# Plain loads with casts on GpSimd, and the first batch transposed by TensorE, in an attention and long-convolution kernel

## Chip, cores, metric

One NeuronCore of a Trainium2 chip. The time is that of one execution on the device, in microseconds (us), as a median of several executions; a profile is one execution with the hardware's records. Some executions are slower than the others whatever the kernel, and are marked slow. The times given are medians of fast runs.

## The reference, cut to what matters

q, k and v are (4 batches, 8 heads, 768 positions, 64), float32. Five heads see only four sink positions and a window of 64; three see every earlier position. The attention output of a batch, 768 x 512, goes through a projection to three parts, a convolution of the middle part with a filter along the sequence, two multiplications and an output projection:

```python
a = softmax(mask(q @ k.T / 8))              # causal, or causal and (sink or window)
x = (a @ v).transpose(0, 2, 1, 3).reshape(4, 768, 512)
x1, x2, x3 = split(x @ w_proj, 3)
x2_conv = irfft(rfft(x2, axis=1) * rfft(filter_fft, axis=0))
out = (x1 * x2_conv * x3) @ w_out           # float32, (4, 768, 512)
```

## The kernel before

The kernel works on pairs: one batch and two heads, 16 in all, four to a batch. A pair needs q and k with the 64 channels on the partitions (`qkT`), and v with positions on the partitions. Scores go through an exponential on ScalarE into `pT`, VectorE multiplies 11 of the 21 blocks of 128 x 128 by a mask of zeros and ones, TensorE multiplies with v (`v_aug`, or `v_far` where v itself is masked). `attn` is transposed into `xT`, and with four pairs done the feed-forward part of that batch (`moe`, with the convolution as matrix products) runs interleaved with the next batch's attention. The parts that the change touches:

```python
def emit_loads(b, hp):
    qk = ald.tile([128, 2, NT, 2, D], BF16, name="qk")
    vf = ald.tile([128, 2, NT, D], FP32, name="v_f32")
    for a, src in ((0, q), (1, k)):
        for hh in range(2):                      # the DMA casts float32 to bfloat16
            nc.gpsimd.dma_start(out=qk[:, a, :, hh],
                in_=src[b, 2 * hp + hh].rearrange("(t p) d -> p t d", p=128))
    nc.sync.dma_start(out=vf, in_=v[b, 2 * hp:2 * hp + 2].rearrange("h (t p) d -> p h t d", p=128))
    return qk, vf
...
def emit_v(st):                                  # cut
    nc.vector.tensor_copy(out=v_aug[:, :, :, 0:64], in_=vf.rearrange("p hh t d -> p t hh d"))
    nc.gpsimd.tensor_mul(v_far, v_aug[:, 0:4], vmask[...])

def emit_prep(st):                               # the crossbar transposes 12 blocks of 128 x 128
    nc.sync.dma_start_transpose(out=qkT.rearrange("p a (t s) -> p (a t) s", t=NT),
                                in_=loads[st["pair"]][0].rearrange("p a t hh d -> p (a t hh d)"))

def emit_turn(st):                               # attn to xT: TensorE for the last pair only,
    if st is state[len(pairs) - 1]: ...          # else the crossbar, 6 blocks
```

"Crossbar" is the DMA transpose. In the code a DMA on `nc.sync` is issued by SyncE (SP), one on `nc.gpsimd` by GpSimd (POOL). A scheduler puts the instructions of each engine into an order, guided by the order of the program.

The softmax here doesn't subtract the row's maximum and nothing guards it: scores larger than these inputs give would overflow.

## Time and profile before

| | before |
|---|---|
| time | 268.87 us (268.46 to 269.48, 3 runs) |
| profiled span | 268.2 us |
| first exponential | 16.61 us |
| feed-forward of batch 0, 1, 2, 3 starts at | 82.4, 135.4, 184.8, 229.3 us |
| granted TensorE clock before the first of these | 0.80 of full speed |
| packets of all DMA queues | 121,523 |

I call the first of these starts **S1**. It divides the kernel: ahead of it transfers bound, behind it TensorE is busy over 90% until the tail. The slices, the chain and the table by stage are in the prediction. One more line sums the first part up. In the page's table of groups, a line has busy time and mean duration before the second bar, and after it the idle time of the engine ahead of these instructions with what ended it:

```profile
L287 PE MATMUL sc<-qkT 64*128 64x512 bf16 (+3 forms) x256 | 37.4, 342 | 42.9 <-DMA qkT<-qk 34.3
```

TensorE stood still for 34.3 us because the transposed q and k had not landed.

### The profile page before, as it was taken

The numbers are of one execution on the slowest core, as the hardware profiler recorded it, in microseconds if no ns is written. First come the engines' busy times: TensorE is split into PE (matmuls) and PEld (weight loads), VectorE is DVE, ScalarE is ACT, GpSimd is POOL, SyncE is SP. The second block draws the span as 40 slices with busy tenths as digits, with TensorE's granted clock in tenths as the row PEclk, the third lists the DMA queues.
The fourth block names the chain that finished last, engine by engine and source line by source line (L and its number), as shares of the span: only waits on it lengthen the run. The fifth ranks groups of instructions, "written<-read, shape, count | busy, mean of one in ns | idle before, by whom it ended". The sixth has DMA issues, their size and how long they took to land.

```text
span 268.2 us, 4095 instructions
## 1 busy us (share of the span) xinstructions
PE 199.7 (74%) x1598; PEld 98.2 (37%) x1598; DVE 153.3 (57%) x290; ACT 152.8 (57%) x182; POOL 80.6 (30%) x118
## 2 busy tenths in 40 slices
PE   0031800729757998998899999999999997999980
PEld 0010500414331434445343455544445462446520
DVE  1329610337743489569944984994397487055640
ACT  1059710445931786766778877768886631664331
POOL 8926940164455155160605426101010000000000
PEclk9999965568955999999999999999999999999997
DMA  8999999999999398999999699748410100410005
GB/s 131 143 172 200 178 169 196 172 163 159 155 180 65 61 148 82 145 142 105 130 302 158 93 136 166 82 87 201 124 29 2 29 4 0 190 47 1 0 7 228
DMA packets 121523, 32.06 MB, mean 120 GB/s; under 512 B 115616, under 2 KB 118432, under 8 KB 121504
## 3 DMA queue, kind: packets, MB, share of 16 engines
q0 software_dynamic: 53072, 9.18, 50.3%
q1 hardware_dynamic: 68432, 22.62, 46.8%
q8 instruction: 12, 0.20, 0.3%
q14 instruction: 7, 0.06, 0.1%
HBM read 24.65 MB, written 6.29 MB: 115 GB/s over the span
## 4 chain that ended last, share of the span: by engine, by line
PE 42%; DVE 21%; DMA 17%; ACT 11%; POOL 4%; issue 3%; ACTq 0%; POOLq 0%; DVEq 0%
DMA qkT<-qk 14%; PE x_ps L378 12%; PE x_ps L346 8%; PE att L313 6%; PE out_ps L407 6%; PE sc L287 5%; ACT pT L293 4%; PE X_ps L216 4%; DVE pT L300 4%; POOL qk L100 3%; DVE conv L399 3%; DVE y L401 2%; DVE conv L400 2%; DVE m L365 2%; DMA xT<-attn 2%
## 5 line engine op out<-in xcount | busy, mean ns | idle before, releaser
L293 ACT ACTIVATE pT<-sc 128x1024 bf16<-128x1024 f32 x96 | 85.8, 923 | 47.1 <-PE sc L287 46.6
L287 PE MATMUL sc<-qkT 64*128 64x512 bf16 (+3 forms) x256 | 37.4, 342 | 42.9 <-DMA qkT<-qk 34.3
L100 POOL DMA_DIRECT2D qk<-in_q_dram x32 | 26.9, 843 | 68.2 <-DMA qkT<-qk 65.0
L378 PE MATMUL x_ps<-xT,wproj 128*128 128x384 bf16 x256 | 46.7, 326 | 0.8 <-ACT X L360 0.8
L300 DVE TENSOR_TENSOR pT<-pT,mask 128x1024 bf16<-128x1024 bf16 x32 | 25.8, 806 | 28.2 <-ACT pT L293 28.2
L313 PE MATMUL att<-v_aug,pT 128*128 128x65 bf16 x352 | 36.3, 206 | 7.3 <-DVE pT L300 4.2
L313 PEld LDWEIGHTS <-pT 128*128 128x128 bf16 x672 | 28.8, 105 | 24.8 <-DVE pT L300 8.4
L287 PEld LDWEIGHTS <-qkT 64*128 64x128 bf16 x256 | 11.8, 98 | 68.7 <-DMA qkT<-qk 34.8
L378 PEld LDWEIGHTS <-wproj 128*128 128x128 bf16 x256 | 23.2, 98 | 16.2 <-issue 3.1
L346 PE MATMUL x_ps<-wproj,xf 128*128 128x512 bf16 x96 | 24.3, 402 | 4.3 <-DVE xf L339 4.2
L100 POOL DMA_DIRECT2D qk<-in_k_dram x32 | 27.0, 850 | 0.2
L407 PE MATMUL out_ps<-wout,y 128*128 128x512 bf16 x96 | 23.9, 381 | 3.8 <-DVE y L401 2.4
L313 PE MATMUL att<-v_far,pT 128*128 128x65 bf16 x320 | 25.9, 206 | 0.0
L216 PE MATMUL X_ps<-x,G 128*128 128x512 bf16 x96 | 23.6, 379 | 0.6 <-ACT X L355 0.3
L268 POOL TENSOR_TENSOR v_far<-v_aug,vmask 128x520 bf16<-128x520 bf16 x16 | 18.8, 1175 | 11.7 <-DVE v_aug L265 11.6
L410 ACT COPY o_sb<-out_ps 128x1024 f32<-128x1024 f32 x12 | 12.2, 1013 | 14.7 <-PE out_ps L407 11.5
L385 ACT CAST x1s<-x_ps 128x768 bf16<-128x768 f32 x16 | 12.8, 800 | 13.5 <-PE x_ps L378 13.5
L349 ACT CAST x<-x_ps 128x1024 bf16<-128x1024 f32 x12 | 12.2, 1014 | 13.0 <-PE x_ps L346 12.8
L365 DVE TENSOR_TENSOR m<-X,HAB 128x1024 bf16<-128x1024 bf16 x12 | 9.8, 815 | 16.1 <-ACT X L355 16.1
L387 DVE TENSOR_TENSOR g<-x1s,x_ps 128x768 bf16<-128x768 bf16 x16 | 15.2, 949 | 6.5 <-PE x_ps L378 5.0
L394 PE MATMUL c_ps<-Gi,P 128*128 128x384 bf16 x96 | 17.6, 326 | 1.5 <-DVE g L387 1.2
L298 DVE TENSOR_TENSOR pT<-pT,mask 128x512 bf16<-128x512 bf16 x16 | 6.7, 416 | 20.0 <-ACT pT L293 20.0
(70 smaller groups left out, 202.8 us busy)
## 6 DMA issues: line engine op xcount, KB each, us to landing
v_f<-in_v_dram SPq DMA_DIRECT2D x16, 384.0 KB, 5.4
out_dram<-o_sb SPq DMA_DIRECT2D x12, 512.0 KB, 2.9
qk<-in_q_dram POOLq DMA_DIRECT2D x32, 96.0 KB, 5.5
qk<-in_k_dram POOLq DMA_DIRECT2D x32, 96.0 KB, 6.2
wproj<-in_moe_w_proj_dram POOLq DMA_DIRECT2D x3, 512.0 KB, 13.1
filt<-in_moe_filter_fft_dram POOLq DMA_DIRECT2D x1, 768.0 KB, 11.4
wout<-in_moe_w_out_dram POOLq DMA_DIRECT2D x1, 512.0 KB, 17.1
qkT<-qk SPq DMA_TRANSPOSE x16, 5.0
```

The costliest lines, as they stand in the source:

```text
L100: nc.gpsimd.dma_start(out=qk[:, a, :, hh], in_=src[b, 2 * hp + hh].rearrange("(t p) d -> p t d", p=128))
L216: nc.tensor.matmul(ps[:, u, :], lhsT=G[:, m, t, :], rhs=src[:, r, m, :], start=(m == 0), stop=(m == NM - 1))
L268: nc.gpsimd.tensor_mul(v_far, v_aug[:, 0:4], vmask[:, hp, :, :, None].to_broadcast([128, 4, 2, 65]))
L287: nc.tensor.matmul(sc[:, hh, n * 128:(n + cnt) * 128], lhsT=qkT[rows, 1, j * 128:(j + 1) * 128], rhs=qkT[rows, 0, i * 128:(i + cnt) * 128] ...
L293: nc.scalar.activation(out=pT[:, :, 512 * c:512 * c + w], in_=sc[:, :, 0:w], func=AF.Exp, scale=SCALE)
L300: nc.vector.tensor_mul(near[:, :, c - 1:c + 1, 0:256], near[:, :, c - 1:c + 1, 0:256], mask[:, h0:h0 + 2, 1, None, :].to_broadcast([128, 2 ...
L313: nc.tensor.matmul(att[:, i, :], lhsT=st["pT"][:, hh, at:at + 128], rhs=st["v_far" if i >= j + 2 else "v_aug"][:, j, hh, :], start=(j == 0 ...
L346: nc.tensor.matmul(ps[:, r, :], lhsT=xf[:, cc, r, m * 128:(m + 1) * 128], rhs=wproj[:, cc, DM:2 * DM], start=(cc == 0), stop=(cc == NC - 1))
L378: nc.tensor.matmul(ps[:, s, 0:HS], lhsT=wproj[:, cc, part * DM + cb * 128:part * DM + (cb + 1) * 128], rhs=xT[:, cc, s * HS:s * HS + HS], ...
L387: nc.vector.tensor_mul(g[:, cb, :].rearrange("p (s t) -> p s t", s=2), x1s, halves[1])
L394: nc.tensor.matmul(ps[:, r, 0:HS], lhsT=P[:, t, u, ch], rhs=Gi[:, :, tile_no, :], start=(n == 0), stop=(n == 2))
L407: nc.tensor.matmul(ps[:, n, :], lhsT=y[:, cb, (i + n) * 128:(i + n + 1) * 128], rhs=wout[:, cb, :], start=(cb == 0), stop=(cb == NC - 1))
```

## The change

Its intent: shorten the first 80 us. Loads of q and k become plain float32 loads from SyncE with GpSimd casting afterwards; for the four pairs of batch 0 the rows are six positions wide (1536 bytes instead of 256) and TensorE transposes q, k and the attention output; the weights are asked for only after the casts of pairs 2, 3 and 4. The diff, cut (the flags of the heads, computed later in the setup, are left out):

```diff
+    def emit_loads(n):
+        qk = ald.tile([128, 2, 2, NT, D], FP32, name="qk_f32")
+        rows = "h (p t) d -> p h t d" if n < BY_PE else "h (t p) d -> p h t d"
+        for dst, src, order in ((qk[:, 0], q, rows), (qk[:, 1], k, rows), (vf, v, "h (t p) d -> p h t d")):
+            nc.sync.dma_start(out=dst, in_=src[b, 2 * hp:2 * hp + 2].rearrange(order, p=128))
+    BY_PE = 4
-    def emit_loads(b, hp):            # four casting loads on GpSimd, v on SyncE
+    def emit_cast(st):
+        for a in range(2):
+            engine = nc.vector if st["n"] == 0 and a == 0 else nc.gpsimd
+            st["cast"] = engine.tensor_copy(out=st["bf"][:, a], in_=qk[:, a].rearrange("p hh t d -> p t hh d"))
     def emit_prep(st):
+        if st["n"] < BY_PE:
+            for a in range(2):
+                ps = bank("qkT_ps", [128, S], BF16)
+                for t in range(NT):
+                    nc.tensor.transpose(ps[:, t * 128:(t + 1) * 128], ..., identity)
+                dst = qkT[:, a].rearrange("d (p t) -> d p t", t=NT)
+                src = ps.rearrange("d (t p) -> d p t", t=NT)
+                # a == 0: copied by VectorE, a == 1: by ScalarE
+            return
         nc.sync.dma_start_transpose(...)
     def emit_v(st):
-        nc.vector.tensor_copy(out=v_aug[:, :, :, 0:64], ...)
+        nc.gpsimd.tensor_copy(out=v_aug[:, :, :, 0:64], ...)
     def emit_turn(st):
-        if st is state[len(pairs) - 1]:
+        if st["n"] < BY_PE or st["n"] == len(pairs) - 1:
     # filter, projection, output weights: issued in pairs 1, 2, 3 instead of 0 and 1, each
+                with tc.issue_after(nxt["cast"].ins):
```

A table load for the sine was moved to the very start as well.

More of the change, by code (lines that the diff above doesn't have):

```diff
@@ L88 @@
     pairs = [(b, hp) for b in range(B) for hp in range(HP)]
-    state.update((n, {"pair": pp}) for n, pp in enumerate(pairs))
+    state.update((n, {"pair": pp, "n": n}) for n, pp in enumerate(pairs))
+    def emit_loads(n):
+        b, hp = pairs[n]
+        qk = ald.tile([128, 2, 2, NT, D], FP32, name="qk_f32")
+        vf = ald.tile([128, 2, NT, D], FP32, name="v_f32")
+        rows = "h (p t) d -> p h t d" if n < BY_PE else "h (t p) d -> p h t d"
+        for dst, src, order in ((qk[:, 0], q, rows), (qk[:, 1], k, rows), (vf, v, "h (t p) d -> p h t d")):
+            nc.sync.dma_start(out=dst, in_=src[b, 2 * hp:2 * hp + 2].rearrange(order, p=128))
+        return qk, vf
@@ L92 @@
+    BY_PE = 4
+    loads = {0: emit_loads(0)}
     ret_i64 = const.tile([128, H], mybir.dt.int64, name="ret_i64")
     nc.sync.dma_start(out=ret_i64, in_=is_retrieval.partition_broadcast(128))
-    def emit_loads(b, hp):
-        qk = ald.tile([128, 2, NT, 2, D], BF16, name="qk")
-        vf = ald.tile([128, 2, NT, D], FP32, name="v_f32")
-        for a, src in ((0, q), (1, k)):
-            for hh in range(2):
-                nc.gpsimd.dma_start(
-                    out=qk[:, a, :, hh], in_=src[b, 2 * hp + hh].rearrange("(t p) d -> p t d", p=128))
-        nc.sync.dma_start(
-            out=vf, in_=v[b, 2 * hp:2 * hp + 2].rearrange("h (t p) d -> p h t d", p=128))
-        return qk, vf
@@ L106, with emit_prep @@
-    PREFETCH = 2
-    loads = {pp: emit_loads(*pp) for pp in pairs[:1]}
+    def emit_cast(st):
+        qk = loads[st["n"]][0]
+        st["bf"] = asb.tile([128, 2, NT, 2, D], BF16, name="qk_bf")
+        for a in range(2):
+            engine = nc.vector if st["n"] == 0 and a == 0 else nc.gpsimd
+            st["cast"] = engine.tensor_copy(out=st["bf"][:, a], in_=qk[:, a].rearrange("p hh t d -> p t hh d"))
+    def emit_prep(st):
+        st["qkT"] = qkT = asb.tile([128, 2, S], BF16, name="qkT")
+        if st["n"] < BY_PE:
+            for a in range(2):
+                ps = bank("qkT_ps", [128, S], BF16)
+                for t in range(NT):
+                    nc.tensor.transpose(ps[:, t * 128:(t + 1) * 128],
+                                        st["bf"][:, a, t].rearrange("p hh d -> p (hh d)"), identity)
+                dst = qkT[:, a].rearrange("d (p t) -> d p t", t=NT)
+                src = ps.rearrange("d (t p) -> d p t", t=NT)
+                if a == 0:
+                    nc.vector.tensor_copy(out=dst, in_=src)
+                else:
+                    nc.scalar.copy(out=dst, in_=src)
+            return
+        nc.sync.dma_start_transpose(
+            out=qkT.rearrange("p a (t s) -> p (a t) s", t=NT),
+            in_=st["bf"].rearrange("p a t hh d -> p (a t hh d)"))
@@ L110 @@
     setup_order = tc.manual_schedule(engines={mybir.EngineType.DVE, mybir.EngineType.Pool})
     setup_order.__enter__()
+    table = const.tile([128, 1], FP32, name="table")
+    nc.vector.memset(table, 0.0)
+    nc.scalar.activation(out=table, in_=table, func=AF.Sin)
     G = const.tile([128, NM, 8, 128], BF16, name="G")
@@ L140 @@
     )
-    ret_w = const.tile([128, 2 * H], FP32, name="ret_w")
-    nc.vector.tensor_scalar(out=ret_w, in0=ret_i64.bitcast(I32), scalar1=0.0, scalar2=None,
-                            op0=ALU.not_equal)
-    ret = const.tile([128, H], FP32, name="ret")
-    nc.vector.tensor_max(ret, ret_w[:, 0:2 * H:2], ret_w[:, 1:2 * H:2])
     nc.gpsimd.affine_select(
@@ L166 @@
                                 op0=ALU.mult)
+    emit_cast(state[0])
     for m in range(NM):
@@ L177 @@
                              scale=-ETA)
+    emit_prep(state[0])
+    ret_w = const.tile([128, 2 * H], FP32, name="ret_w")
+    nc.vector.tensor_scalar(out=ret_w, in0=ret_i64.bitcast(I32), scalar1=0.0, scalar2=None,
+                            op0=ALU.not_equal)
+    ret = const.tile([128, H], FP32, name="ret")
+    nc.vector.tensor_max(ret, ret_w[:, 0:2 * H:2], ret_w[:, 1:2 * H:2])
     if n_sink:
@@ L261, in emit_v @@
     def emit_v(st):
-        vf = loads.pop(st["pair"])[1]
+        vf = loads.pop(st["n"])[1]
         st["v_aug"] = v_aug = asb.tile([128, NT, 2, 65], BF16, name="v_aug")
         nc.gpsimd.memset(v_aug[:, :, :, 64:65], 1.0)
-        nc.vector.tensor_copy(out=v_aug[:, :, :, 0:64], in_=vf.rearrange("p hh t d -> p t hh d"))
+        nc.gpsimd.tensor_copy(out=v_aug[:, :, :, 0:64], in_=vf.rearrange("p hh t d -> p t hh d"))
         st["v_far"] = v_far = asb.tile([128, 4, 2, 65], BF16, name="v_far")
@@ L268, in emit_v @@
         nc.gpsimd.tensor_mul(v_far, v_aug[:, 0:4], vmask[:, hp, :, :, None].to_broadcast([128, 4, 2, 65]))
-    def emit_prep(st):
-        st["qkT"] = qkT = asb.tile([128, 2, S], BF16, name="qkT")
-        nc.sync.dma_start_transpose(
-            out=qkT.rearrange("p a (t s) -> p (a t) s", t=NT),
-            in_=loads[st["pair"]][0].rearrange("p a t hh d -> p (a t hh d)"))
     def emit_chunk(st, c):
@@ L413, in moe @@
             yield
-    emit_prep(state[0])
+    emit_v(state[0])
     emit_mask(0)
     emit_mask(1)
-    emit_v(state[0])
     setup_order.__exit__(None, None, None)
-    loads[pairs[1]] = emit_loads(*pairs[1])
+    loads[1] = emit_loads(1)
     gates = []
@@ L448 @@
             if c == (0 if n < 2 else 3) and n + 2 < len(pairs):
-                loads[pairs[n + 2]] = emit_loads(*pairs[n + 2])
+                loads[n + 2] = emit_loads(n + 2)
             if c == 0 and last:
@@ L453 @@
                 emit_values(last, 1)
-            if c == (1 if n else 3) and nxt:
+            if c == 1 and nxt:
+                emit_cast(nxt)
+                emit_v(nxt)
+                if n + 1 >= BY_PE:
+                    emit_prep(nxt)
+            if c == 3 and n + 1 < BY_PE:
                 emit_prep(nxt)
-                emit_v(nxt)
             if c == 2 and last:
@@ L460 @@
                 gates.append(moe(b - 1, last["xT"]))
-            if c == 1 and n == 0:
+            if c == 1 and n == 1:
                 filt = msb.tile([128, NT, DM], BF16, name="filt", tag="xf")
-                nc.gpsimd.dma_start(out=filt, in_=moe_filter_fft.rearrange("(t p) c -> p t c", p=128))
-            if c == 1 and n == 1:
+                with tc.issue_after(nxt["cast"].ins):
+                    nc.gpsimd.dma_start(out=filt, in_=moe_filter_fft.rearrange("(t p) c -> p t c", p=128))
+            if c == 1 and n == 2:
                 w = moe_w_proj.rearrange("(c p) n -> p c n", p=128)
-                for part in (1, 0, 2):
-                    cols = slice(part * DM, part * DM + DM)
-                    nc.gpsimd.dma_start(out=wproj[:, :, cols], in_=w[:, :, cols])
-                nc.gpsimd.dma_start(out=wout, in_=moe_w_out.rearrange("(c p) n -> p c n", p=128))
+                with tc.issue_after(nxt["cast"].ins):
+                    for part in (1, 0, 2):
+                        cols = slice(part * DM, part * DM + DM)
+                        nc.gpsimd.dma_start(out=wproj[:, :, cols], in_=w[:, :, cols])
+            if c == 1 and n == 3:
+                with tc.issue_after(nxt["cast"].ins):
+                    nc.gpsimd.dma_start(out=wout, in_=moe_w_out.rearrange("(c p) n -> p c n", p=128))
             if c < 5:
```

## The prediction

> **What bounds the kernel now.** I read the page first (its slices and queue table), then the chain that ended last, then busy time by stretch, then the timeline where two engines meet. The slices show two different kernels in one:
>
> ```profile
> PE   0031800729757998998899999999999997999980
> PEclk9999965568955999999999999999999999999997
> DMA  8999999999999398999999699748410100410005
> ```
>
> A slice is 6.7 us. For twelve slices (80 us) the DMA engines are full and TensorE is not; from slice 13 on TensorE is at 80 to 99%. Its granted clock is also low, 5 to 8 tenths, in most of slices 6 to 13. The chain says what the first part waits for:
>
> ```profile
> 15.21 12.42 DMA qkT<-qk
> ...
> 32.61 15.78 DMA qkT<-qk
> ...
> 50.29 8.91 DMA qkT<-qk
> ...
> 76.54 4.74 DMA xT<-attn
> ...
> 82.39 3.61 PE x_ps L346 x8
> ```
>
> Three waits for the transposed q and k of pairs 1, 2 and 3 (a pair is one batch and two heads) take 12.4 + 15.8 + 8.9 = 37.1 us of the chain; they include the load and the cast that the transpose waits for. The feed-forward part of batch 0 can start only at 82.4 us. The later starts of that part, from the same chain, are 135.6, 184.9 and 229.5 us, so I cut the span there:
>
> ```profile
> core 0: us, PE busy (x) PEld busy (x) DVE busy (x) ACT busy (x) POOL busy (x), PEclk, DMA share, GB/s
> 0.00:16.00 16.00, 0.04 (x2) 0.04 (x4) 3.14 (x10) 1.28 (x1) 13.63 (x28) 1.00 1.38 141
> 16.00:82.40 66.40, 30.69 (x279) 16.82 (x280) 32.93 (x69) 34.58 (x41) 30.55 (x41) 0.75 1.66 173
> 82.40:135.60 53.20, 49.28 (x412) 23.17 (x413) 38.18 (x67) 36.42 (x44) 19.31 (x26) 0.96 1.16 113
> 135.60:184.90 49.30, 47.18 (x418) 22.94 (x417) 36.03 (x69) 36.78 (x45) 15.93 (x22) 1.00 1.02 151
> 184.90:229.50 44.60, 41.84 (x333) 20.04 (x332) 27.85 (x52) 27.89 (x34) 1.21 (x2) 1.00 0.20 39
> 229.50:268.20 38.70, 30.70 (x160) 15.19 (x158) 15.18 (x25) 15.85 (x19) 0.00 (x0) 0.95 0.21 80
> ```
>
> In the second row no engine reaches 53%, and the DMA share is 1.66 (over 1 because packets of two queues overlap). In rows three to five TensorE is busy 93 to 96%. So **only the first 82 us can be shortened by better transfers**; the other 186 us belong to TensorE. What the transfers are:
>
> ```profile
> q0 software_dynamic: 53072, 9.18, 50.3%
> q1 hardware_dynamic: 68432, 22.62, 46.8%
> qk<-in_q_dram POOLq DMA_DIRECT2D x32, 96.0 KB, 5.5
> qkT<-qk SPq DMA_TRANSPOSE x16, 5.0
> ```
>
> Nearly all packets are of 256 bytes or less. Per pair: q and k 4 x 768 = 3072 packets, v 1536. From the hardware queue's total (68432, less 16 x 1536 for v and 12 x 256 for the stores, over 306 blocks of 128 x 128) a transposed block costs 133 packets, so qkT (12 blocks) is about 1600 and xT (6) about 800. Together about 7000 a pair.
>
> **The Trainium skill.** (1) "DMA: Bandwidth & Descriptors", Specifications, wants at least 512 bytes per transfer for line rate. The trace agrees: from 60 to 80 us it moved 17325 small packets, 866 per us, at 163 GB/s; from 40 to 50 us, when weights passed, 1452 packets of 1024 written bytes and 1928 small ones moved 194 GB/s as written, and the weights are read at twice that width, so some 340 GB/s as read. (2) "SBUF — State Buffer", Who interferes with whom: a VectorE instruction with two SBUF inputs, or in a two-port mode, and a GpSimd instruction that reads SBUF lock each other out whole. The trace agrees:
>
> ```profile
> 118.41 2.06 DVE L300 TENSOR_TENSOR pT<-pT,mask 128x1024 bf16<-128x1024 bf16 x1 [1.95 <-ACT pT L293]
> 118.84 1.07 POOL L268 TENSOR_TENSOR v_far<-v_aug,vmask 128x520 bf16<-128x520 bf16 x1
> ```
>
> The mask multiplication takes 0.69 us in the median of 32 and 2.06 beside v_far. (3) "GPSIMD Engine Reference", section 3.1: about 2.6 cycles per element with two inputs, 1.03 to 1.8 with one. v_far (520 elements, two inputs) at 1.08 us is 2.5 cycles at 1.2 GHz; the copy of G (384 elements, one input) took 0.56 to 0.60 us. (4) "TensorE: Matmul & The Clock Gate", Part 1: idle windows of 3.4 us halve the clock. The trace agrees: 0.50 from 40 to 50 us, where TensorE was busy 1.56 of 10 us.
>
> **The change, part by part.**
>
> Removed: 64 casting loads on GpSimd (0.85 us of issue each, 54 us), 16 casts of v on VectorE (0.55 each, 8.8 us), four crossbar transposes of qk and four of attn.
>
> Added on GpSimd: 31 casts of q or k and 16 of v, 768 elements each. By the copy of G, less 0.15 us of start, 0.43/384 us per element; 768 of them and the start give 1.0 us. 47 x 1.0 = 47 us against 54 removed, but now reading SBUF. Added for batch 0: 48 + 24 TensorE transposes (0.22 us each singly, six in 0.50 us), 4 copies of 768 from PSUM on VectorE and 4 on ScalarE (0.80 by the cast of x1s), 4 of xT on VectorE (0.55).
>
> *Packets up to 82 us.* Before: from the stretches 57,200 packets. In the changed kernel a batch-0 pair has 2 x 2 x 128 = 512 packets of 1536 bytes for q and k, 786 KB, 2.3 us at 340 GB/s, and 1536 of v, 1.8 us at 866 per us: 4.1 us against 7000/866 = 8.1. What must pass before the feed-forward part can start: four pairs 16.4; the matrix Gi (24 blocks, 3200 packets) 3.7; filter and projection 2304 packets of 2 KB, 4.7 MB read, 13.9; q, k and v of pairs 4 and 5, 2 x 4608/866 = 10.6; qkT of pair 4, 1.8. Sum 46.4 us, from about 1 us on: **a DMA floor of 47 us** for a start that is now at 82.4.
>
> *Start.* Without DMA issues GpSimd's constants end near 4 us; q and k, issued first on SyncE, should land by 4.5 to 5 (2 us of latency by the 3 to 3.5 us of the fastest landings, and 2.3 of transfer); cast to 6; six transposes each; then the copies of qkT: VectorE's after its angles near 8.3, ScalarE's after four sines near 10.3. The table of exponentials (1.28) then puts the first exponential at 11.6, against 16.61.
>
> *Pairs 0 to 3 and half of 4.* ScalarE does most: a pair has five exponentials of 0.95, one of 0.4 and a copy of 0.85: 6.0. Four pairs 24, HAB's four evacuations 4, four chunks of pair 4 4: 32 us. In pair 2 of the kernel before, undisturbed from 48.4 to 55.9, ScalarE was busy 5.1 of 7.5 us, 70%; with a warmer clock I take 75 to 80%: 40 to 43 us, so the start falls at 52 to 54. It is above the DMA floor, but close. I choose **52.5** for 82.4: 29.9 us gained.
>
> *From there to the last start (147.1 us).* The first period, 53.2, still held DMA waits; I take 50.3, like the next: 2.9 gained. GpSimd now reads SBUF 4.1 us a pair where it did 1.1: 12 pairs x three more casts, half of which meet a two-input VectorE instruction for half a microsecond: 9 us of VectorE, less 6.6 us of casts of v taken off it. VectorE is at 72 to 73% there, so a third of the new waits may reach TensorE: 3 lost. Zero together. The tail, 38.7 us, has neither loads nor GpSimd: unchanged.
>
> Sum: 268.9 - 29.9 - 2.9 + 3 = **239 us**.
>
> **The rivals.** *A: the transfers still bound.* Batches 1 to 3 keep 256-byte rows, and pairs 4 to 6 load just while the weights pass. For it: the floor of 47 us against 52.5 is thin; SyncE now issues all loads and transposes in order, so a transpose that waits for a cast holds the loads behind it, and loads ahead fill its queue. Against: 12.5 us a pair later leaves room for 8.1. If so, the start falls at 60 and the time is 246 to 250. *B: GpSimd or its lock becomes the bound.* For it: the 2.06 us above; the cast feeds the transpose that feeds the next pair. Against: 4.2 us of GpSimd per 12.5 us pair. If casts take 2 us rather than 1 and VectorE's waits all reach TensorE, 10 to 15 us are lost: 250. *C: the gain is larger*, because ScalarE runs at 90% while nothing is cold, and the DMA floor binds at 47: 232.
>
> **Range and chances.** A and B are the likelier misses, hence the longer upper side: 230 to 250. For "within 2%" the time must exceed 263.5, so 24 of 30 us must be lost again; the 37 us of waits are too plain for that. Faster 0.95, same 0.04, slower 0.01.
>
> **What would show each step.** First exponential near 11.6 us; no wait over 3 us for qkT in pairs 1 to 3; the x2 matmuls' first start between 50 and 55; granted clock over 0.85 before it; later starts 49 to 51 us apart; casts on GpSimd 1.0 us in the median, v_far and the mask multiplication with more long cases. The prediction is wrong if qkT<-qk_bf or casts take the old place in the chain after pair 4, if SyncE's own waits hold loads, or if TensorE falls under 90% between the starts.

## The result, and the profile after

| | before | after |
|---|---|---|
| time, median (range) | 269.18 us (268.46 to 269.55, a fourth run added) | 247.45 us (246.36 to 248.33, 4 runs) |
| ratio | 1 | 0.9194, interval 0.9151 to 0.9237 |
| profiled span | 268.2 us | 245.6 us |
| first exponential | 16.61 us | 12.01 us |
| S1 and the later starts | 82.4, 135.4, 184.8, 229.3 | 58.6, 112.7, 162.5, 206.6 |
| from S1 to the end | 185.8 us | 187.0 us |
| clock before S1 | 0.80 | 0.91 |
| packets | 121,523 | 101,299 |

A ratio is the mean time of one kernel's fast runs over that of the other's of the same rounds, so not quite the ratio of the medians quoted. The result is correct.

The whole gain is ahead of S1 (23.8 us earlier); from S1 on 1.2 us are lost. The slices of the changed kernel's page, 6.1 us each:

```profile
PE   1428667976996999989999999899999979999880
PEclk9999985798999799999999999999999999999998
DMA  7969999999999999999998552383102003300015
```

TensorE works from the second slice on, where it had been mostly idle for seven; the clock falls to 7 tenths or less only in slices 7, 8 and 14. But the DMA engines stay nearly full for 22 slices, 135 us: the changed kernel still has transfers to make all that time. The table by stage, with the same columns as in the prediction:

```profile
12.00:58.60 46.60, 31.78 (x330) 17.66 (x328) 35.37 (x63) 30.47 (x35) 22.41 (x29) 0.89 1.10 200
58.60:112.70 54.10, 50.35 (x409) 23.74 (x413) 35.14 (x62) 36.03 (x44) 20.77 (x26) 0.94 1.21 210
112.70:162.50 49.80, 47.07 (x413) 23.05 (x419) 34.53 (x64) 36.85 (x45) 17.98 (x23) 1.00 0.72 150
162.50:206.60 44.10, 41.19 (x331) 19.93 (x333) 27.60 (x51) 27.75 (x34) 2.78 (x4) 1.00 0.18 40
206.60:245.60 39.00, 30.31 (x159) 15.27 (x159) 15.17 (x25) 16.01 (x20) 0.00 (x0) 0.97 0.21 81
```

Ahead of S1 no engine is a bound by its own busy time: TensorE 68%, VectorE 76%, ScalarE 65%, GpSimd 48%. And the wait for transposed q and k has gone. This line answers to the one shown of before, then follow the transposes that remain and the new casts:

```profile
L310 PE MATMUL sc<-qkT 64*128 64x512 bf16 (+3 forms) x256 | 36.2, 335 | 2.0 <-ACT pT L316 1.2
...
L113 POOL CAST qk_bf<-qk_f 128x768 bf16<-128x768 f32 x31 | 28.0, 910 | 47.5 <-DMA qk_f<-in_q_dram 22.5
...
qkT<-qk_bf SPq DMA_TRANSPOSE x12, 4.6
```

42.9 us of idle time ahead of the scores have become 2.0. The chain that ended last (start, duration, what) now passes ahead of S1 from engine to engine, in pieces of a few us; the only long one is a row of masks on VectorE:

```profile
13.72 3.87 DVE mask L223 x5
17.59 1.19 DVE pT L321
...
57.25 1.29 DVE xf L362
59.03 2.58 PE x_ps L369 x6
```

### The profile page after: what moved, and what is told of

It is laid out like the page before. It is cut to its first block, busy times and chain, and to the rows that moved or that the text cites. A ratio compares the mean times of both kernels' runs of the same rounds, so it can differ in the third digit from the quotient of the medians.

```text
span 245.6 us, 4173 instructions
## 1 busy us (share of the span) xinstructions
PE 203.7 (83%) x1656; PEld 101.6 (41%) x1670; DVE 155.7 (63%) x284; ACT 154.7 (63%) x186; POOL 70.7 (29%) x101
## 2 busy tenths in 40 slices
DMA packets 101299, 35.99 MB, mean 147 GB/s; under 512 B 93344, under 2 KB 98208, under 8 KB 101280
## 4 chain that ended last, share of the span: by engine, by line
PE 48%; DVE 30%; ACT 12%; DMA 4%; issue 3%; SPq 1%; POOL 0%; ACTq 0%; DVEq 0%
PE x_ps L401 13%; PE x_ps L369 9%; PE X_ps L245 7%; PE att L336 6%; PE out_ps L430 6%; DVE pT L323 6%; PE sc L310 5%; ACT pT L316 5%; DVE y L424 3%; DVE conv L422 3%; DMA qk_f<-in_q_dram 2%; DVE P L391 2%; DVE m L390 2%; DVE conv L423 2%; DVE mask L223 2%
## 5 line engine op out<-in xcount | busy, mean ns | idle before, releaser
L336 PE MATMUL att<-v_aug,pT 128*128 128x65 bf16 x352 | 34.4, 202 | 10.0 <-DVE pT L321 4.7
L113 POOL CAST qk_bf<-qk_f 128x768 bf16<-128x768 f32 x31 | 28.0, 910 | 47.5 <-DMA qk_f<-in_q_dram 22.5
L336 PEld LDWEIGHTS <-pT 128*128 128x128 bf16 x672 | 27.5, 102 | 25.8 <-issue 7.8
L310 PE MATMUL sc<-qkT 64*128 64x512 bf16 (+3 forms) x256 | 36.2, 335 | 2.0 <-ACT pT L316 1.2
L430 PE MATMUL out_ps<-wout,y 128*128 128x512 bf16 x91 | 22.8, 381 | 5.7 <-DVE conv L423 3.7
L336 PE MATMUL att<-v_far,pT 128*128 128x65 bf16 x320 | 24.9, 202 | 0.0
L310 PEld LDWEIGHTS <-qkT 64*128 64x128 bf16 x256 | 10.6, 96 | 27.0 <-issue 23.7
L297 POOL TENSOR_TENSOR v_far<-v_aug,vmask 128x520 bf16<-128x520 bf16 x16 | 20.1, 1261 | 0.7
L344 DVE TENSOR_TENSOR attn<-att,rec 128x384 bf16<-128x384 f32 x32 | 17.8, 555 | 0.9
L293 POOL MEMSET v_aug<- 128x12 bf16 x16 | 2.5, 154 | 54.0 <-PE att L336 54.0
```

Source lines behind the costliest of these rows:

```text
L113: st["cast"] = engine.tensor_copy(out=st["bf"][:, a], in_=qk[:, a].rearrange("p hh t d -> p t hh d"))
L297: nc.gpsimd.tensor_mul(v_far, v_aug[:, 0:4], vmask[:, hp, :, :, None].to_broadcast([128, 4, 2, 65]))
L310: nc.tensor.matmul(sc[:, hh, n * 128:(n + cnt) * 128], lhsT=qkT[rows, 1, j * 128:(j + 1) * 128], rhs=qkT[rows, 0, i * 128:(i + cnt) * 128] ...
L336: nc.tensor.matmul(att[:, i, :], lhsT=st["pT"][:, hh, at:at + 128], rhs=st["v_far" if i >= j + 2 else "v_aug"][:, j, hh, :], start=(j == 0 ...
L344: nc.vector.tensor_mul(st["attn"][:, :, hh, :], att[:, :, 0:64], rec[:, :, None].to_broadcast([128, NT, 64]))
L430: nc.tensor.matmul(ps[:, n, :], lhsT=y[:, cb, (i + n) * 128:(i + n + 1) * 128], rhs=wout[:, cb, :], start=(cb == 0), stop=(cb == NC - 1))
```

## The experiments

Twelve kernels ran, each three rounds (five_and_masks_late five), each beside runs of the kernel before. All are edits of the changed kernel. "S1" is read from the profile of each, one execution; differences of S1 under about 1 us aren't taken as effects. The spans of one kernel's fast runs differ by up to 3.7 us (masks_late, 244.1 to 247.8), so a difference of S1 of 2 to 4 us that the time doesn't show as well is weak. One run each of all_crossbar (266.20) and narrow_rows (249.20) was slow and is left out.

| kernel | time, us | ratio to before | S1 | from S1 on |
|---|---|---|---|---|
| after | 247.45 | 0.9194 | 58.6 | 187.0 |
| all_crossbar | 261.74 | 0.9689 | 74.6 | 184.8 |
| turn_xbar | 255.70 | 0.9488 | 69.0 | 184.8 |
| narrow_rows | 245.88 | 0.9091 | 62.1 | 184.4 |
| weights_early | 248.92 | 0.9228 | 61.3 | 187.1 |
| casting_pe | 252.54 | 0.9369 | 63.7 | 187.1 |
| masks_late | 248.13 | 0.9196 | 59.7 | 188.1 |
| five_and_masks_late | 247.22 | 0.9168 | 58.3 | 187.3 |
| casts_twice | 255.99 | 0.9485 | 59.5 | 196.5 |
| memsets_extra | 250.85 | 0.9289 | 63.7 | 185.8 |
| casts_write_only (wrong) | 243.49 | 0.9006 | 58.9 | 183.3 |
| v_on_dve | 247.45 | 0.9205 | 60.8 | 184.7 |
| wide_all (wrong order) | 254.95 | 0.9445 | 59.0 | 194.8 |

My theory: the crossbar's packets and waits were the cost, and what remains above the prediction is the pace of the four first pairs. Rivals: transfers still bind S1 (A of the prediction); the lock between GpSimd and VectorE gives part of the gain back (B).

### Where the gain came from

**all_crossbar**: loads, casts and late weights as changed, but no TensorE transposes and no wide rows.

```diff
-    BY_PE = 4
+    BY_PE = 0
```

> Undoes one part: batch 0 goes by 256-byte rows and the crossbar too, as in the kernel before; plain loads, casts on GpSimd and the late weights stay. Two theories of why the feed-forward part of batch 0 starts at 58.6 us and not at the 52.5 predicted. Transfers theory (the DMA engines still bind the first part): 20,000 packets more come ahead of that start (4 pairs x 2560 for q and k, 1600 for qkT, 800 for xT), at 866 per us 23 us of DMA, less 9 us for the wide packets that they replace: the start falls near 72 us and the time near 261 us. Lock theory (VectorE and GpSimd block each other, the transfers are mostly hidden now): the start falls at 61 to 65 us, time 250 to 253 us.

S1 is 74.6, time 261.74 us, much as the transfers theory had it. So of the 23.8 us by which S1 fell, 16.0 belong to the work of batch 0 taken off the crossbar, with its row width, and 7.8 to the rest. The waits show the old picture again:

```profile
PEld L310 <- DMA qkT<-qk_bf: 30.3, 5, 11.3
```

(total us, times, longest: the weight loads of the scores waited five times for transposed q and k.)

**turn_xbar**: q and k by TensorE, but the attention output of batch 0 by the crossbar.

```diff
-        if st["n"] < BY_PE or st["n"] == len(pairs) - 1:
+        if st["n"] == len(pairs) - 1:
```

> The change as it is, but the transposes of batch 0's attention output stay with the crossbar, as in the kernel before; q and k of batch 0 still go over TensorE. Theory 'two PSUM banks pace batch 0' (attention values, xT and qkT share them, and TensorE waited 0.81 and 1.76 us for the copies of xT): TensorE works with fewer waits, feed-forward of batch 0 starts at 56 to 57, time 245 to 246. Theory 'transfers pace batch 0': 4 x 800 packets more, at the 57200/82 = 700 per us of the kernel before 4.6 us, and a transpose that waits for the attention of a pair holds the loads behind it in SyncE's order: feed-forward starts at 61 to 64, time 250 to 253. If neither binds: 58.6 and 247.

S1 is 69.0 and the time 255.70 us: worse than either theory gave. Four transposes of `attn` cost 10.4 us of S1, over twice the 4.6 us of their packets. The chain shows how:

```profile
30.21 13.16 DMA xT<-attn
...
64.03 3.95 DMA xT<-attn
```

and SyncE's own timeline (start, duration of the issue) shows the order:

```profile
34.56 7.91 SPq L99 DMA_DIRECT2D qk_f<-in_q_dram  x1
42.57 8.75 SPq L355 DMA_TRANSPOSE xT<-attn  x1
51.49 1.41 SPq L130 DMA_TRANSPOSE qkT<-qk_bf  x1
```

The issue of a load takes 7.9 us here, where the next load of q, at 57.3 us, takes 0.59; the transpose behind it takes 8.75, and the q and k of pair 4, whose transpose the changed kernel issues at 44.6, wait until 51.5. SyncE issues without a gap from 28 to 69 us. The attention outputs do not hold it up, contrary to the expectation: they were ready at 24.8, 31.1, 46.0 and 59.5 us on VectorE's timeline, and SyncE came to their transposes at 30.2, 42.6, 54.7 and 64.0. VectorE in turn had to wait, once, until the first transpose gave a buffer of `attn` back (total us, times, longest):

```profile
DVE attn L344 <- DMA xT<-attn: 6.1, 1, 6.1
```

So the gain of taking `attn` off the crossbar is not its own packets alone but the place that it had in SyncE's order.

**narrow_rows**: TensorE transposes from ordinary 256-byte rows.

```diff
-        rows = "h (p t) d -> p h t d" if n < BY_PE else "h (t p) d -> p h t d"
+        rows = "h (t p) d -> p h t d"
-                dst = qkT[:, a].rearrange("d (p t) -> d p t", t=NT)
-                src = ps.rearrange("d (t p) -> d p t", t=NT)
+                dst, src = qkT[:, a], ps
```

> Undoes only the row size: batch 0 is still transposed by TensorE, but from 256-byte rows, so its copies of qkT out of PSUM are plain as well. Transfers theory: 4 pairs x 2560 packets more, 11.8 us of DMA for the 9.2 us less that the bytes cost in wide packets... net about 4 to 6 us later start (63 to 65 us), time 251 to 254 us. Lock theory: the loads are hidden, and the plain copies out of PSUM gain a few tenths each: time 246 to 248.5 us.

The packets up to S1 rise by a third, in the DMA view of the changed kernel and then of this one:

```profile
DMA packets 29681, 12.28 MB, mean 209 GB/s; under 512 B 24814, under 2 KB 29678, under 8 KB 29678
```

```profile
DMA packets 39288, 12.11 MB, mean 195 GB/s; under 512 B 36469, under 2 KB 39285, under 8 KB 39285
```

The bytes are nearly the same, the rate falls by 7% and S1 comes 3.5 us later, where the chain now leads through the transpose of pair 4 (40.70 to 54.68 us). The time is no longer, if anything shorter: 245.88 against 247.45 us, ratio 0.905 to 0.9131 against 0.9151 to 0.9237. The two were not run in the same rounds, so whether the wide rows cost that one per cent is not settled. In the profile, what S1 lost was made good in the next period, 51.3 us against 54.1. The wide rows, for which the prediction counted 2.3 us for q and k of a pair where 3072 packets at its 866 per us take 3.5, gain nothing in the end.

**weights_early**: the weights asked for in pairs 0 and 1, with no wait for a cast.

```diff
-            if c == 1 and n == 1:
+            if c == 1 and n == 0:          # filter
-                with tc.issue_after(nxt["cast"].ins):
```

> Undoes only the place of the weights: the filter is issued at pair 0, projections and output matrix at pair 1, without the order behind the casts (the scheduler puts the filter ahead of all casts, about 2 us into the program). Transfers theory: 4.2 us of filter traffic now lies ahead of or beside the first q and k, so the first exponential is 2 to 4 us later than 12.0 and pair 3 waits for 10 us of projections: time 250 to 254 us. Lock theory: the early part has room in the queues, time 246 to 249 us.

The first exponential comes at 20.06 instead of 12.01 us. q of the first pair was cast at 4.03 us, as early as in the changed kernel (4.05). What comes late beside the filter is q of the second pair, issued at 4.63, and here GpSimd's order has its cast ahead of that of k of the first pair, which starts at 16.21. The chain shows it:

```profile
4.63 10.18 DMA qk_f<-in_q_dram
...
14.87 0.82 POOL qk_bf L113
```

In the changed kernel that load lands 5.79 us after its issue, and GpSimd casts k of the first pair before it, at 5.19.

S1 is only 2.7 us later, and the ratios' intervals overlap (0.9195 to 0.9262 against 0.9151 to 0.9237). Of eight microseconds at the start most are absorbed: the first sign that S1 hangs on several chains.

**casting_pe**: the casting loads on GpSimd of the kernel before, v cast on VectorE, but TensorE transposes and late weights. The rows are narrow too, and the weights wait for the first mask multiplication, as there is no cast to wait for.

```diff
+                nc.gpsimd.dma_start(out=qk[:, a, :, hh], in_=...)   # four a pair, casting
-            st["cast"] = engine.tensor_copy(...)                     # no casts on GpSimd
+        nc.vector.tensor_copy(out=v_aug[:, :, :, 0:64], ...)
```

> Undoes the loads and casts alone: q and k come by the casting loads of the kernel before (256-byte rows, issued by GpSimd), v is cast on VectorE, no GpSimd cast is left; TensorE's transposes in batch 0 and the later weights stay. The narrow rows cost nothing in an earlier run, so what differs is plain load plus cast against casting load. Lock theory: 16 v_far reads are all that GpSimd reads, so VectorE runs free: 240 to 245 us if the casting loads carry the traffic. Transfers theory (small casting packets are slower: before the change 53072 of them took 50% of the DMA engines' span against 47% for 68432 of the plain queue): the first part loses 5 us or more, time 250 to 256 us.

First exponential at 17.70, S1 at 63.7, time 252.54 us: plain loads with casts are worth some 5 us over casting loads, as the transfers theory said, and with either the larger part of the gain is there.

### What bounds S1 at 58.6

**masks_late**: the masks for the heads of pairs 1 to 3 are computed after the first mask multiplication of the pair before.

```diff
         if b == 0 and hp + 1 < HP:
-            emit_mask(2 * hp + 2)
-            emit_mask(2 * hp + 3)
...
             emit_chunk(st, c)
+            if c == 0 and n + 1 < HP:
+                with tc.issue_after(st["first"].ins):
+                    emit_mask(2 * hp + 2)
+                    emit_mask(2 * hp + 3)
```

> The change as it is, but the masks of the heads of pairs 1 to 3 are computed after the first mask multiplication of the pair before, no longer all ahead of the first one. In the changed kernel seven masks in a row (4.97 us of VectorE, 12.62 to 17.59) stand between the first exponentials and the first mask multiplication at 17.5, and TensorE waits for it. Theory 'VectorE's masks hold the first pair': the first multiplication comes near 14.5, feed-forward of batch 0 starts 3 us earlier (55.6 instead of 58.6), time 244 to 245, ratio 0.908. Rival 'what paces pairs 1 to 4 is something later (two PSUM banks, the clock, the transfers)': the 3 us at the start are waited out again, the start of feed-forward stays within 1 us of 58.6, time 246.5 to 248.

The first multiplication comes 4.3 us earlier, at 13.23 us on VectorE's timeline, where the changed kernel had 17.51. S1 is 59.7: nothing gained. The rival was right (within 0.1 us), and the chain shows what had stood behind the masks:

```profile
16.93 1.07 POOL v_far L297
...
31.97 12.39 DMA qk_f<-in_q_dram
44.36 8.87 DMA qkT<-qk_bf
```

First, TensorE now waits for the masked v of pair 0. GpSimd computes it only after the casts of pairs 1 and 2, and did so in the changed kernel too. These are the two engines there, VectorE's mask multiplication and GpSimd's masked v, which end within a microsecond of one another:

```profile
17.51 1.27 DVE L321 TENSOR_TENSOR pT<-pT,mask 128x512 bf16<-128x512 bf16 x1
```

```profile
17.32 2.37 POOL L297 TENSOR_TENSOR v_far<-v_aug,vmask 128x520 bf16<-128x520 bf16 x2
```

The wait there was put down to VectorE, which came last; GpSimd would have ended it hardly sooner. Secondly, from 32 us on the chain goes through the load of q of pair 5 and then the crossbar transpose of pair 4, whose first half is worked on ahead of S1. Pair 4's casts were done at 36.5 us, but SyncE had first to issue the load of k of pair 5, which took it 10.47 us, and could issue the transpose only at 44.36. That is rival A, by way of SyncE's order.

**five_and_masks_late**: as masks_late, and pair 4 gets wide rows and TensorE transposes too (its attention output stays with the crossbar).

```diff
-    BY_PE = 4
+    BY_PE = 5
-        if st["n"] < BY_PE or st["n"] == len(pairs) - 1:
+        if st["n"] < HP or st["n"] == len(pairs) - 1:
```

> The kernel with the masks of pairs 1 to 3 computed later, and besides pair 4, whose first part is worked on ahead of the feed-forward part of batch 0, gets 1536-byte rows and transposes on TensorE (its attention output stays with the crossbar). With the masks later, the chain led through the load of q (31.97 to 44.36) and the crossbar transpose of pair 4 (issued at 44.36, landed at 53.23), which stood behind the load of k of pair 5 in SyncE's order; TensorE waited 3.3 us for it. Theory 'two chains of nearly equal length end at the start of feed-forward, VectorE's masks and the transfers for pair 4': with both shortened the start comes 2 to 3.5 us earlier than 58.6, at 55 to 56.6, ratio to before 0.905 to 0.91, time 244 to 245. Rival 'TensorE's cold clock and the two PSUM banks pace it': the waits move elsewhere, the start is 58 to 60, ratio 0.918 to 0.922, 247 to 248. A third: fewer packets early let weights and later loads arrive earlier, the period after the start is shorter too: under 243.

S1 is 58.3 and the ratio 0.9168 (0.914 to 0.9196): the rival again, though the transfer chain is now out of the way. The chain to S1 of this run:

```profile
17.58 1.08 POOL v_far L297
...
38.84 1.74 DVE fold L258
40.62 2.72 PE X_ps L245 x6
...
52.56 2.91 ACT pT L316 x3
55.50 0.98 DVE pT L323
56.48 0.48 DVE xT L353
```

It passes GpSimd, VectorE, TensorE, ScalarE and VectorE again. So S1 has at least three chains of nearly equal length: VectorE's masks, GpSimd's casts ahead of `v_far`, and the transfers of pair 4. Shortening one, or two, uncovers the next. The work itself had not changed: casts_twice, below, added 6.8 us of VectorE busy time ahead of 58.5 us and moved S1 by 0.9, so VectorE's sum of work is no bound either; the order of the waits is. Which single step would have to move next is not settled; relieving GpSimd at 11 to 18 us together with the masks and the transfers was not run. Nor were two rivals from the expectations isolated, TensorE's clock and the two PSUM banks that `att`, `xT` and `qkT` share. In the changed kernel the clock was 0.72 to 0.77 from 30 to 50 us; of TensorE's 14.8 us of idle time between 12.0 and 58.6 us, waits of the transposes for a copy of `xT` out of a bank make up 2.6 us.

### The lock between GpSimd and VectorE

Three kernels have the same order of instructions on TensorE, ScalarE and VectorE as the changed kernel, and differ in what GpSimd does.

**casts_twice**: every GpSimd cast is done a second time into a spare tile (reads doubled).

```diff
+            if engine is nc.gpsimd:
+                nc.gpsimd.tensor_copy(out=spare, in_=qk[:, a].rearrange("p hh t d -> p t hh d"))
+        nc.gpsimd.tensor_copy(out=spare, in_=vf.rearrange("p hh t d -> p t hh d"))
```

> Each of the 47 GpSimd casts is followed by a second one of the same source into a spare tile: 47 x 0.83 us = 39 us more of reading on GpSimd, nothing more on other engines, same order there. Lock theory: half of the added reads hold up VectorE by half their length, some 8 to 15 us of VectorE's waits, half of which reach TensorE: time 251 to 256 us. Order theory: GpSimd has time to spare (29% busy), so 247 to 249 us.

**memsets_extra**: in place of the second cast a memset of the same size (writes only).

```diff
+                nc.gpsimd.memset(spare, 0.0)
+        nc.gpsimd.memset(spare, 0.0)
```

> The control for the doubled casts: after each cast a memset of a spare tile of the same size on GpSimd, which writes and doesn't read. Lock theory: two-input instructions of VectorE are not held up by it[...], so time 247 to 249 us, clearly under the doubled casts. If instead GpSimd's own length is what counts (the casts come later, so qkT comes later), this is as slow per added microsecond as the doubled casts.

**casts_write_only**: each GpSimd cast becomes a memset and a cast of one column, so the result is wrong.

```diff
+            nc.gpsimd.memset(st["bf"][:, a], 0.01)
+            st["cast"] = nc.gpsimd.tensor_copy(out=st["bf"][:, a, 0, 0, 0:1], in_=qk[:, a, 0, 0, 0:1])
```

> A wrong result on purpose: the 47 GpSimd casts become a memset of the same tile and a copy of one column (which still waits for the load), so GpSimd writes the tiles but hardly reads. The instructions of TensorE, ScalarE and VectorE and their order are the same as in the changed kernel. Lock theory (a GpSimd instruction that reads SBUF holds up VectorE's two-input instructions): the long cases of the mask multiplication become few, the masks at 12.6 us take 3 us instead of 5, the feed-forward part starts at 54 to 56 us instead of 58.6, time 241 to 244 us. Rival, order theory (the first part is set by the fixed order on TensorE and its cold clock): start within 1 us, time 246 to 248 us.

From S1 to the end, after has 187.0 us. With 47 more casts (0.83 us each where nothing holds them, 39 us of reading) it is 196.5; with 47 memsets (of 0.74, 35 us of writing) 185.8; with the casts' reads nearly gone 183.3. GpSimd's busy time alone costs nothing there; its reads do. Ahead of S1 they cost nothing: casts_write_only has S1 at 58.9, where the lock theory gave 54 to 56. (The time of memsets_extra is 3.4 us longer, but all of it is ahead of S1: its chain there goes through a load of k, issued at 25.02 us and landed 17.92 us later, and the transpose of pair 4 again. SyncE's order of loads differs there too; how the memsets brought this about is not shown.) The durations of VectorE's multiplications between 59 and 206 us show the lock, first those of two products in the changed kernel:

```profile
L424 DVE TENSOR_TENSOR y<-conv,g 128x768 bf16<-128x768 bf16 x12 | 8.5, 709 | 0.0
...
L390 DVE TENSOR_TENSOR m<-X,HAB 128x1024 bf16<-128x1024 bf16 x9 | 7.5, 834 | 0.1
```

then without GpSimd's reads:

```profile
L428 DVE TENSOR_TENSOR y<-conv,g 128x768 bf16<-128x768 bf16 x12 | 6.6, 550 | 0.0
...
L394 DVE TENSOR_TENSOR m<-X,HAB 128x1024 bf16<-128x1024 bf16 x9 | 6.1, 678 | 0.7 <-ACT X L387 0.7
```

and with them doubled:

```profile
L394 DVE TENSOR_TENSOR m<-X,HAB 128x1024 bf16<-128x1024 bf16 x9 | 9.2, 1023 | 1.2 <-ACT X L387 1.2
```

and with the memsets beside the casts:

```profile
L394 DVE TENSOR_TENSOR m<-X,HAB 128x1024 bf16<-128x1024 bf16 x9 | 6.7, 740 | 0.1
```

A product of 1024 elements takes 678 ns in the mean with hardly any reads beside it, 834 with the casts and 1023 with them twice. Such a mean counts how many of nine products met a read, not only how many reads there are: with the memsets it is 740 at the same casts, and in the kernel before, where GpSimd reads little more than for `v_far`, 849. One by one (18 products of this form in each kernel) they take 0.65 to 0.69 us, beside a memset too, and 0.94 to 1.54 us only where a GpSimd cast or `v_far` runs beside: 5 in the changed kernel, none in casts_write_only, 2 in memsets_extra, 8 in casts_twice. Steadier is VectorE's busy time in the whole span, for the same 284 instructions: 147.9 us in casts_write_only, 155.7 in the changed kernel, 156.4 in memsets_extra, 171.1 in casts_twice. (Behind S1 the second casts add 7.8 us to VectorE's time, 120.2 instead of 112.4, and 9.5 us to the kernel's. They also hold the loaded tile longer, which a memset does not; what that adds was not separated.)

"SBUF — State Buffer", Who interferes with whom, of the Trainium skill, names just this case, a VectorE instruction with two SBUF inputs against a GpSimd instruction that reads; the runs agree, and they add a price: 3.7 us behind S1 for 47 casts of 0.83 us, and 4.0 us by the whole times (243.49 against 247.45 us; the fast runs don't overlap). The part behind S1 varies by itself between 184.4 and 188.1 us among the kernels that cast everything on GpSimd once and keep the narrow rows of batches 1 to 3, so the price may be anything from 1.1 to 4.8 us; the 9.5 of the doubled casts stands well clear of that. It is no argument for the casting loads: casting_pe, without a cast on GpSimd, needs 187.1 us there.

**v_on_dve**: v cast on VectorE again, 16 of GpSimd's 47 casts gone.

```diff
-        nc.gpsimd.tensor_copy(out=v_aug[:, :, :, 0:64], in_=vf.rearrange("p hh t d -> p t hh d"))
+        nc.vector.tensor_copy(out=v_aug[:, :, :, 0:64], in_=vf.rearrange("p hh t d -> p t hh d"))
```

> The change as it is, but v is cast on VectorE as in the kernel before: 16 of GpSimd's 47 casts, 16 x 0.83 us, leave GpSimd, and VectorE does 16 x 0.55 us more. Theory 'the lock is what casts on GpSimd cost': the kernel whose GpSimd casts only wrote gained 4.0 us on all 47 less one column each, so a third of that, 1.3 us, comes back, less what VectorE's 8.8 us cost where it is on the path (VectorE is at 65 to 70% there, some 2 us): 246 to 249, same. Theory 'VectorE is the bound after 58 us': all 8.8 us show, less 1.3: 254. Theory 'the order of GpSimd's work (casts of q, k, then v, then v_far) delays the values': v ready earlier, 244.

The same time, 247.45 us, made up otherwise: S1 2.2 us later, 2.3 us less from S1 on. The order of TensorE's and VectorE's work changed too, so the 2.3 us are not the lock's alone.

### Fewer packets for all pairs

**wide_all**: all pairs get the wide rows. For batches 1 to 3 the crossbar then puts the positions in the wrong order. (The comparison with the reference still called the output correct. With q and k of a tenth the scores are near zero and the attention weights nearly even, which may be why; the kernel is not a correct one.)

```diff
-        rows = "h (p t) d -> p h t d" if n < BY_PE else "h (t p) d -> p h t d"
+        rows = "h (p t) d -> p h t d"
```

> A wrong result on purpose: q and k of all pairs are loaded in 1536-byte rows (512 packets for 3072), though only batch 0 is put back in order; so the later batches are attended in a permuted order. No engine's work changes. Transfers theory: pairs 4 to 6 cost 3 us less of DMA each, so the first feed-forward start falls from 58.6 to 53 to 55 us and the next period (54.5 us now) shrinks by 2 to 4: time 239 to 243 us. Lock theory: start within 1 us of 58.6 and time 246 to 248 us.

70,579 packets instead of 101,299, and 7.5 us slower. Neither theory. S1 is the same, but the next period takes 60.3 us. GpSimd's casts wait there for the transposes, and the transposes are issued once in about 12 us:

```profile
POOL qk_bf L113 <- DMA qkT<-qk_bf: 78.4, 10, 9.7
```

```profile
68.44 3.04 SPq L130 DMA_TRANSPOSE qkT<-qk_bf  x1
80.81 2.81 SPq L130 DMA_TRANSPOSE qkT<-qk_bf  x1
92.86 2.55 SPq L130 DMA_TRANSPOSE qkT<-qk_bf  x1
```

In the changed kernel the same wait sums to 19.6 us in 6 times. With loads that the scheduler takes for quicker, it put SyncE's and GpSimd's instructions into another order, and a ring closed: a cast waits for the transpose of two pairs back (there are two `qk_bf` buffers), the cast of v stands behind it in GpSimd's order, the next load of v waits for that cast's buffer, and the next transpose stands behind that load in SyncE's order. The ring is read from the two engines' timelines and waits; no run broke it with the packets held fixed, so it is argued, not proven.

## Why the prediction was right or wrong

It was right in its verdict and its range (230 to 250), and 8.5 us low in its number. By its steps:

**The start** was right: first exponential predicted at 11.6, measured at 12.01 us. Not foreseen were the seven masks that keep the first mask multiplication until 17.51 us; by masks_late they cost nothing in the end.

**The waits for transposed q and k** were right as the cause. The idle time ahead of the scores fell from 42.9 to 2.0 us, and all_crossbar brought waits of 30 us back with 14.3 us of time. How much of it belonged to the attention output was not foreseen: turn_xbar alone costs 8.25 us of time.

**"Pairs 0 to 3 and half of 4"** is the step that failed, and in one term. ScalarE's work was predicted at 32 us and was 30.47 us between 12.0 and 58.6. But the share "75 to 80%" was taken from one undisturbed stretch of the kernel before (70%) and raised for a warmer clock; it was 30.47 of 46.60, 65%. A busy share of 65% instead of 75 to 80% makes 46.6 us of these 30.47 instead of 38 to 41, and S1 58.6 instead of 52.5: 6.1 of the miss. Choosing one engine and a share for it was the error, because no engine ran near its limit. The runs show in its place several chains of waits across the engines, close behind one another: 4.3 us taken from the first moved S1 by nothing, and a relief of the second neither.

**The DMA floor** of 47 us was too low as a floor for what TensorE needs: in masks_late q and k of pair 4 landed at 53.2 us, in narrow_rows at 54.7. It summed packets as if they could pass in the order in which they are needed, 24,512 in all; ahead of S1 29,681 passed, those of later pairs among them, and SyncE issues the transpose of pair 4 at 44.6 us behind a load of pair 5 whose issue took 8.42 us.

**From S1 on** the prediction said zero, as 2.9 gained and 3 lost. Measured: 1.2 lost. Without the reads it is 183.3 against 185.8 before, 2.5 gained; the reads cost 3.7. Both sums are near, but within a spread of 3.7 us between kernels, and by luck in part. The lock's mechanism held, but with the reads VectorE is busy 4.9 us longer behind S1 (112.4 and 107.7), where 9 were counted, and most of that reached the end of the kernel, where a third was counted. The first period was misjudged, 54.1 instead of 50.3 us: without the reads it is 51.8, so only 1.2 us of the gain fall there and not 2.9, and 2.3 of the lock's 3.7. The casts took 0.83 us in the median, not 1.0.

**The rivals.** A gave "60 and 246 to 250", and its numbers are the nearest to what came. Its mechanism is real but is not alone: with pair 4 off the crossbar and the masks moved, S1 stayed. B's mechanism is real and its size is some 4 us, not 10 to 15. C is refuted: ScalarE was at 65%, not 90%. Of the prediction's own signs of being wrong one came true: SyncE's issues held loads and a transpose, for up to 8.42 us.

In the sum: the prediction took 29.8 us off, the profile shows 22.6; the 7.2 us between are 6.1 from S1 and 1.1 from the part behind it. The remaining microsecond is that the median of the changed kernel lies 1.85 us above its profiled span, that of the kernel before 1.0, because the run of it that was profiled, 269.9 us, was longer than its median.

**Slips in the working** that change nothing: up to 82.4 us 59,302 packets passed in the kernel before, not 57,200, ScalarE's 5.04 of 7.5 us in pair 2 are 67% and not 70, and TensorE reaches 80% from slice 14 on, not 13.

## What to carry to other kernels

A transfer that is waited for costs what stands before it in the issuing engine's order, not only its own packets; taking short transposes off a full queue gained more here than its packets say, and making rows six times wider gained nothing. When the one long wait is gone, don't size the remainder by one engine's work at a guessed share: look for the second and third chain behind the longest, because removing the first is worth only the distance to the next. A cast moved to GpSimd was paid here by VectorE's two-input instructions while it read (4.9 us of VectorE's time behind S1, some 4 us of the kernel's); count the reads, not GpSimd's busy time.

## What the Trainium skill lacked or had wrong

- "DMA: Bandwidth & Descriptors", Specifications, asks for transfers of at least 512 bytes. An overhead for each small packet stands further down on that page, not what it is worth in a kernel. Here rows of 1536 instead of 256 bytes for four of 16 pairs, 29,681 instead of 39,288 packets ahead of S1, went with 209 instead of 195 GB/s and did not shorten the time: 247.45 us with them, 245.88 without.
- "Perfetto Trace Analysis", What "DMA-bound" means, names an issuing engine whose track is solid with DMA slices as a bound, but gives no duration and does not say that the same issue can take very different times: in the changed kernel SyncE issued without a gap from 15.5 to 62 us; a plain load of 384 KB in rows of 256 bytes took it 8.42 us to issue at 36.0 us and another of the same form 0.70 us at 51.3, and a transpose that was needed stood behind the first.
- "TensorE: Matmul & The Clock Gate", Part 4, gives about 390 ns for a 128 x 128 transpose alone and 275 in a kernel. In the changed kernel six in a row took 0.50 to 0.51 us or, in four of seven cases with q and k, 0.80 to 0.82, so 0.08 to 0.14 us for each: the page's durations should not be added up.
- "SBUF — State Buffer", Who interferes with whom, was right on reads against writes; it has no figure for a whole kernel. Here 47 casts that read cost about 4 us, as many again 9.5, and 35 us of added writes nothing behind S1.
